# The activation of the second MoE: its series kept in the PSUM bank of h, with one SBUF input per VectorE operation

## The chip, the cores and the metric

The kernel runs on one core of a Trainium2 chip. The metric is the device time of one execution in microseconds (us), taken as the median of several runs. One execution was also recorded by the hardware profiler; all rows below come from that one. A core has TensorE (PE, matmuls; PEld is its weight loads), VectorE (DVE), ScalarE (ACT), GpSimd (POOL) and SyncE (SP, which issues DMAs). TensorE writes its results to PSUM, which has eight banks of 512 fp32 columns. In this kernel VectorE and ScalarE read and write PSUM, and GpSimd works on SBUF alone.

## The reference

An RWKV-like attention over 4 x 768 tokens feeds a first MoE with eight experts (top one of eight, ReLU), and its output x of 3072 tokens x 384 goes through a second dense block, which the change concerns:

```
def _moe2_ref(x, w_in, w_out):          # x 3072x384, w_in 384x2048, w_out 2048x384
    h = x @ w_in
    g = h - np.tanh(h)
    return (g @ w_out).astype(np.float32)
```

## The kernel before, in words

The program runs its stages one after the other: attention, routing, first MoE, second MoE. Within a stage each engine has its own queue of instructions, in the order in which the code writes them, and semaphores hold an instruction until what it needs is there.

The second MoE treats the tokens in NBK = 6 blocks (j) of BK = 512 and the 2048 hidden columns in CH2 = 16 chunks (f) of 128. So there are 96 chunks, i = 16 j + f. Matrices are held as a rounded part and a remainder ("hi" and "lo"), and a product takes three passes: hi with hi, and the two mixed ones. For chunk i:

- nm1(i), L1229: nine matmuls of 512 columns into h, one whole PSUM bank (pool psh, three banks).
- in the same function ScalarE computes z = h squared (L1233), tanh(h) into t (L1235), s (L1237) and mk (L1239), which is the ReLU of z - 0.16 and serves as a mask.
- gfun(i), five VectorE operations. For small h, tanh cancels, so a series in z is used there: L1245 w = h z; L1246 t = tanh(h) - h; L1247 and L1248 multiply w by two factors, from s and from z; L1249 puts t over w where the mask is set. All values are negative g; the sign is turned at the output.
- gsplit(i): ScalarE casts w to the hi part of g (L1264), GpSimd subtracts for the lo part (L1265).
- nm2(i, q, pass), L1276: for four token tiles q, three passes, twelve matmuls of 384 columns into the accumulators o (pool pso, five banks).

Step i of the loop writes, in this order: in three steps of a block (f = 10, 11, 12) xsplit, which prepares the next block's tokens (a ScalarE cast L904, a subtraction L905); gsplit(i + 1); nm1(i + 3); in the first eight steps w_split, which prepares the last weights (L84 on ScalarE, L85 on GpSimd); nm2; at a block's end o_copy (L1282 on VectorE for the first tile, L1284 on ScalarE for the others); gfun(i + 3); in four steps of a block a scatter of the block before (L1289, an indirect DMA that GpSimd issues). In the last block four nm2 are held back (HELD), to be done after the loop. After the loop the remaining nm2 run in two parts, tile by tile, and behind each tile of the second part stand its o_copy and scatter.

Three banks of h mean that nm1(i + 3) writes the bank of chunk i and waits until its last reader has ended. That is L1246 here, the second operation of gfun. The tiles z, t, s, mk and w have two buffers each.

Before the second MoE, the first one has a "decode" (L936 to L943), which unpacks the second MoE's weights on VectorE, partly in a PSUM tile of 384 columns named dec: L938 reads and writes dec in place, L940 reads it and writes SBUF.

Of the kernel before, what the change touches and what calls it, by code (L numbers as in the profile page):

```python
# [8 lines left out]
F32 = mybir.dt.float32  # L9
# [3 lines left out]
U32 = mybir.dt.uint32  # L13
U64 = mybir.dt.uint64
ACTF = mybir.ActivationFunctionType
ALU = mybir.AluOpType
# [6 lines left out]
G_T = 0.4  # L23
G_A = 2.6447346478370597
G_B = -0.0715155286080183
G_D = 6.5360647804198555
G_K = 0.01926817304071779
# [3 lines left out]
def rwkv_moe_moe_kernel(ctx: ExitStack, tc: tile.TileContext, rk_t, rkv, pk, u, wp1, wp2, out):  # L31


    nc = tc.nc
    B, C, P, _, H, D = rkv.shape
# [43 lines left out]
    def w_split(p, part, eng=nc.vector):  # L79
        half, n = part // 2, 384  # L80
        sl = slice(part * n, (part + 1) * n)
        of = stg[p, half][:, part % 2 * n:(part % 2 + 1) * n]
        dst = ring[p % RING]
        nc.scalar.copy(out=dst[:, 0, sl], in_=of)  # L84
        eng.tensor_tensor(out=dst[:, 1, sl], in0=of, in1=dst[:, 0, sl].bitcast(F32), op=ALU.subtract)  # L85
        if part % 2:
            stg.pop((p, half))

    def w1_of(i):
        p, c = divmod(i, 2)  # L90
        W = ring[p % RING]
        return lambda s, kk: W[:, s, kk * 256 + c * P:kk * 256 + (c + 1) * P]
# [39 lines left out]
    gt2 = const.tile([P, 1], F32, name="gt2")  # L132
# [11 lines left out]
    def consts():  # L144
        nc.gpsimd.memset(ones16, 1.0)
        nc.gpsimd.memset(gb, G_K ** 0.5 * G_B)
        nc.gpsimd.memset(gt2, -G_T * G_T)
        nc.gpsimd.tensor_copy(out=ltri, in_=mlt)
        nc.gpsimd.iota(out=iotaf, pattern=[[1, P]], base=-P, channel_multiplier=0,
                       allow_small_or_imprecise_dtypes=True)  # L150
        nc.gpsimd.iota(out=pid, pattern=[[1, 1]], base=0, channel_multiplier=1,
                       allow_small_or_imprecise_dtypes=True)
        nc.gpsimd.iota(out=e8, pattern=[[-1, E]], base=E, channel_multiplier=0,
                       allow_small_or_imprecise_dtypes=True)
        nc.gpsimd.iota(out=thr, pattern=[[P, 4]], base=0, channel_multiplier=0,
                       allow_small_or_imprecise_dtypes=True)
        nc.gpsimd.iota(out=q1, pattern=[[1, 4]], base=1, channel_multiplier=0,
                       allow_small_or_imprecise_dtypes=True)
        nc.gpsimd.iota(out=ide, pattern=[[1, E]], base=0, channel_multiplier=0,
                       allow_small_or_imprecise_dtypes=True)  # L160
        nc.gpsimd.iota(out=iov, pattern=[[P, QOV]], base=0, channel_multiplier=0,
                       allow_small_or_imprecise_dtypes=True)
        for e in range(E):
            nc.gpsimd.memset(capv[:, e:e + 1], float(CAPS[e]))

        nc.gpsimd.iota(out=tie, pattern=[[-1, E]], base=0, channel_multiplier=0,
                       allow_small_or_imprecise_dtypes=True)
        nc.gpsimd.memset(tie[:, 0:1], float(2 * N * E))

        nc.gpsimd.iota(out=tileid, pattern=[[P, NT]], base=0, channel_multiplier=0,  # L170
                       allow_small_or_imprecise_dtypes=True)
# [489 lines left out]
    with tc.manual_schedule():  # L661
# [101 lines left out]
        for q in range(2):  # L763
            t = ps1.tile([P, HP, P], F32, tag=f"A{q}", name=f"hp{q}").rearrange("p j t -> p (j t)")
# [129 lines left out]
    BK = 512  # L894
# [3 lines left out]
    def x_tile(name):  # L898
        return xbp.tile([P, 2, KD, BK], F32R, tag="xb", name=name)

    def xsplit(j, d, eng=nc.vector):
        if d == 0:
            xb[j] = x_tile("xb")
        nc.scalar.copy(out=xb[j][:, 0, d, :], in_=Y[d][:, j * BK:(j + 1) * BK])  # L904
        eng.tensor_tensor(out=xb[j][:, 1, d, :], in0=Y[d][:, j * BK:(j + 1) * BK],  # L905
                          in1=xb[j][:, 0, d, :].bitcast(F32), op=ALU.subtract)
# [234 lines left out]
    with tc.manual_schedule():  # L1141
# [7 lines left out]
        for i in range(NC1):  # L1149
# [9 lines left out]
            e, f = divmod(i, CH1)  # L1159
# [8 lines left out]
            for t in range(*((max(k, 0) * NT // S0) for k in (i - CH1, i - CH1 + 1))):  # L1168
                if t < NT:
                    nc.gpsimd.indirect_dma_start(  # L1170
                        out=permd, out_offset=bass.IndirectOffsetOnAxis(ap=pos[:, t:t + 1], axis=0),
                        in_=tok[:, t:t + 1], in_offset=None)
            if i == CH1 + S0 + 2:
                nc.gpsimd.dma_start(out=perm, in_=permd.rearrange("(i p) o -> p (i o)", p=P))
            if i == CH1 + S0 + 4:
# [3 lines left out]
                                        op0=ALU.logical_shift_right, op1=ALU.bitwise_and)  # L1179
                nc.vector.tensor_scalar(out=pc, in0=perm, scalar1=9, scalar2=7,  # L1180
                                        op0=ALU.logical_shift_right, op1=ALU.logical_shift_left)
# [23 lines left out]
    hz, gg, ops, osb = {}, {}, {}, {}  # L1205
    m2 = ctx.enter_context(ExitStack())
    with tc.manual_schedule():

        wl = x_tile("wl").rearrange("p s k t -> p (s k t)").bitcast(F32)
        for k in range(LATE):  # L1210
            w = wl[:, k * 1536:(k + 1) * 1536]
# [4 lines left out]
    gsp = m2.enter_context(tc.tile_pool(name="gsp", bufs=2))  # L1216
# [5 lines left out]
    def nm1(i):  # L1222
        j, f = divmod(i, CH2)
        wf = w1_of(NC1 + f)
        ps = psh.tile([P, BK], F32, tag="h", name="h")
        n = 0
        for kk in range(KD):
            for a, b in PASS:
                nc.tensor.matmul(ps, lhsT=wf(a, kk), rhs=xb[j][:, b, kk, :], start=(n == 0), stop=(n == 8))  # L1229
                n += 1  # L1230

        z = gsp.tile([P, BK], F32, tag="z", name="z")
        nc.scalar.activation(out=z, in_=ps, func=ACTF.Square)  # L1233
        t = gsp.tile([P, BK], F32, tag="t", name="t")
        nc.scalar.activation(out=t, in_=ps, func=ACTF.Tanh)  # L1235
        s = gsp.tile([P, BK], F32, tag="s", name="s")
        nc.scalar.activation(out=s, in_=z, func=ACTF.Square, scale=G_K ** 0.5, bias=gb)  # L1237
        mk = gsp.tile([P, BK], F32, tag="mk", name="mk")
        nc.scalar.activation(out=mk, in_=z, func=ACTF.Relu, bias=gt2)  # L1239
        hz[i] = ps, z, s, t, mk  # L1240

    def gfun(i):
        ps, z, s, t, mk = hz.pop(i)
        ww = gsp.tile([P, BK], F32, tag="w", name="w")
        nc.vector.tensor_tensor(out=ww, in0=ps, in1=z, op=ALU.mult)  # L1245
        nc.vector.tensor_tensor(out=t, in0=t, in1=ps, op=ALU.subtract)  # L1246
        nc.vector.scalar_tensor_tensor(out=ww, in0=s, scalar=G_K * G_D, in1=ww, op0=ALU.add, op1=ALU.mult)  # L1247
        nc.vector.scalar_tensor_tensor(out=ww, in0=z, scalar=G_A, in1=ww, op0=ALU.subtract, op1=ALU.mult)  # L1248
        nc.vector.copy_predicated(out=ww, mask=mk.bitcast(U32), data=t)  # L1249
        gg[i] = ww  # L1250

    def g_buf(i):

# [7 lines left out]
    def gsplit(i):  # L1261
        ww = gg[i]
        g = gg[i] = g_buf(i)
        nc.scalar.copy(out=g[:, 0, :], in_=ww)  # L1264
        nc.gpsimd.tensor_tensor(out=g[:, 1, :], in0=ww, in1=g[:, 0, :].bitcast(F32), op=ALU.subtract)  # L1265
# [27 lines left out]
    with tc.manual_schedule():  # L1293
        NC2 = NBK * CH2
        done = 0
        for i in range(LEAD):
            if i == LEAD - 1:
                gsplit(0)
            nm1(i)
            gfun(i)  # L1300
        for i in range(NC2):
            j, f = divmod(i, CH2)
            if f in (10, 11, 12) and j + 1 < NBK:
                xsplit(j + 1, f - 10, nc.gpsimd if j == 0 else nc.vector)
            if i + 1 < NC2:
                gsplit(i + 1)
            if i + LEAD < NC2:
                nm1(i + LEAD)
            if i < 4 * LATE:
                w_split(NP1 + NP2 - LATE + i // 4, i % 4, eng=nc.gpsimd)  # L1310
            if j < NBK - 1 or (f not in HELD and i + LEAD < NC2):

                if f == 0:
                    for q in range(NQ2):
                        nm2(done, q, (0, 1))
                    for q in range(NQ2):
                        nm2(done, q, (2,))
                elif f == CH2 - 1:
                    for q in range(NQ2):
                        nm2(done, q, (0, 1, 2))  # L1320
                    o_copy(j, 0, True)
                else:
                    for n in range(3):
                        for q in range(NQ2):
                            nm2(done, q, (n,))
                done += 1
            if i + LEAD < NC2:
                gfun(i + LEAD)
            if f == CH2 - 1 and j < NBK - 1:
                for q in range(1, NQ2):  # L1330
                    o_copy(j, q, False)
            if j > 0 and f in (1, 2, 3, 4):
                scatter(j - 1, f - 1)

        for part in (range(done, NC2 - 2), range(NC2 - 2, NC2)):
            for q in range(NQ2):
                for i in part:
                    nm2(i, q, (0, 1, 2))
                if part[-1] == NC2 - 1:
                    o_copy(NBK - 1, q, q % 2 == 0)  # L1340
                    scatter(NBK - 1, q)
# [50 lines left out]
```

## Time and profile before

| | us |
|---|---|
| median of 3 runs | 853.72 (852.47 to 856.5) |
| profiled execution | 846.33 |
| its span, first to last instruction | 844.6 |
| PE busy / PEld busy | 793.5 (94%) / 702.8 (83%) |
| DVE busy | 716.6 (85%) |
| ACT busy / POOL busy | 529.5 (63%) / 442.9 (52%) |

The span is what lies between the first and the last instruction of the profiled execution. PE's busy time is modelled from matmuls that overlap each other; the starts of its weight loads, one for each matmul, show its pace better. Shares are means over stages which have different limits, so what counts is read stage by stage. The second MoE's first matmul is at 410.40 us.

### The profile page before, as it was taken

To read this page: it belongs to the slowest core of one execution; us is meant where nothing else is said; L and a number is where in the kernel's file an instruction comes from. 1 tells how busy PE (TensorE), PEld (TensorE's weight loads), DVE (VectorE), ACT (ScalarE), POOL (GpSimd) and SP (SyncE) were. 2 spreads that over 40 slices of the span, in tenths; PEclk is the share of its full clock that TensorE was granted. 3 is DMA by queue.
4 is the path that set the end of the run, shared out by engine and by line. 5 is a ranking of instruction groups with operands and counts; after the bars stand their busy time and mean duration, and the time that the engine had idled before them with its cause. 6 is when DMAs were issued, how large, how long until landed. Compare 5 with 4: busy or idle time off the path is not lost.

```text
span 844.6 us, 14609 instructions
## 1 busy us (share of the span) xinstructions
PE 793.5 (94%) x5052; PEld 702.8 (83%) x5052; DVE 716.6 (85%) x1139; ACT 529.5 (63%) x1135; POOL 442.9 (52%) x426
## 2 busy tenths in 40 slices
PE   8799999899999899998998989999999999999985
PEld 7567777798899899998977779989989989988875
DVE  7798887459867869896499999999999999999992
ACT  7778786336444435544566676777777677677660
POOL 6997785237577677666344534325325334334433
PEclk8999999999999999999999999999999999999998
DMA  8978863246688799885200000000000000000000
GB/s 220 272 213 222 255 183 105 84 129 197 184 268 238 207 250 285 241 238 136 88 1 1 1 10 29 1 0 38 1 1 38 1 0 29 10 1 19 20 1 37
DMA packets 34982, 89.91 MB, mean 106 GB/s; under 512 B 5690, under 2 KB 13022, under 8 KB 34896
## 3 DMA queue, kind: packets, MB, share of 16 engines
q1 hardware_dynamic: 30704, 78.87, 32.6%
q0 software_dynamic: 4192, 9.99, 3.7%
q8 instruction: 42, 0.69, 0.3%
q14 instruction: 44, 0.36, 0.1%
HBM read 73.10 MB, written 15.74 MB: 105 GB/s over the span
## 4 chain that ended last, share of the span: by engine, by line
DVE 27%; issue 11%; ACT 7%; PE 7%; POOL 1%; DVEq 0%; POOLq 0%; ACTq 0%
DVE w L1247 12%; DVE w L1248 6%; DVE w L1245 5%; PE h L1229 3%; DVE w L1249 2%; PE o L1276 2%; ACT mk L1239 2%; PE y L1004 1%; ACT z L1233 1%; ACT g L1264 1%; ACT s L1237 1%; PE hps L979 1%; ACT t L1235 1%; ACT xb L904 1%; DVE xb L905 1%
## 5 line engine op out<-in xcount | busy, mean ns | idle before, releaser
L1265 POOL TENSOR_TENSOR g<-w,g 128x512 fp32r<-128x512 f32 x93 | 121.7, 1308 | 232.5 <-ACT g L1264 220.4
L1229 PE MATMUL h<-xb,ring 128*128 128x512 f32 x864 | 217.6, 396 | 6.6 <-DVE xb L905 3.5
L1276 PE MATMUL o<-ring,g 128*128 128x384 f32 x1116 | 211.6, 338 | 6.9 <-ACT g L1264 3.9
L1276 PEld LDWEIGHTS o<-ring,g 128*128 128x128 f32 x1116 | 195.8, 188 | 19.4 <-ACT g L1264 8.0
L1229 PEld LDWEIGHTS h<-xb,ring 128*128 128x128 f32 x864 | 160.7, 188 | 40.1 <-DVE xb L905 5.2
L1247 DVE SCALAR_TENSOR_TENSOR w<-s,w 128x512 f32<-128x512 f32 x96 | 138.4, 1441 | 0.0
L85 POOL TENSOR_TENSOR ring<-stg,ring 128x384 fp32r<-128x384 f32 x102 | 105.3, 1057 | 47.8 <-ACT ring L84 38.6
L1264 ACT CAST g<-w 128x512 fp32r<-128x512 f32 x93 | 57.9, 622 | 110.4 <-DVE w L1249 110.4
L1004 PE MATMUL y<-h,ring 128*128 128x256 f32 (+7 forms) x576 | 115.5, 345 | 1.3 <-DVE h L983 1.1
L979 PE MATMUL hps<-xt,ring 128*128 128x472 f32 (+6 forms) x504 | 107.1, 355 | 5.8 <-DVE xt L968 3.1
L1004 PEld LDWEIGHTS y<-h,ring 128*128 128x128 f32 x576 | 102.2, 190 | 5.2 <-DVE h L983 1.4
L84 ACT CAST ring<-stg 128x384 fp32r<-128x384 f32 x152 | 71.8, 511 | 55.3 <-DMA stg<-in_wp_dram 40.4
L979 PEld LDWEIGHTS hps<-xt,ring 128*128 128x128 f32 x504 | 90.8, 189 | 10.9 <-DVE xt L968 3.7
L1249 DVE COPY_PREDICATED w<-mk,t 128x512 f32<-128x512 uint32 x96 | 80.1, 835 | 9.9
L1248 DVE SCALAR_TENSOR_TENSOR w<-z,w 128x512 f32<-128x512 f32 x96 | 68.4, 713 | 3.3
L1245 DVE TENSOR_TENSOR w<-h,z 128x512 f32<-128x512 f32 x96 | 65.3, 680 | 6.8 <-ACT t L1235 6.8
L1237 ACT ACTIVATE s<-z,gb 128x512 f32<-128x512 f32 x96 | 69.5, 724 | 0.0
L1239 ACT ACTIVATE mk<-z,gt 128x512 f32<-128x512 f32 x96 | 69.2, 721 | 0.0
L1246 DVE TENSOR_TENSOR t<-t,h 128x512 f32<-128x512 f32 x96 | 65.2, 679 | 0.0
L1233 ACT ACTIVATE z<-h 128x512 f32<-128x512 f32 x96 | 57.2, 595 | 11.1 <-PE h L1229 10.1
L344 ACT ACTIVATE am<-ident,dt 128x128 f32<-128x128 f32 x192 | 58.6, 390 | 4.9 <-DVE dt L337 4.5
L983 DVE SCALAR_TENSOR_TENSOR h<-hps,h 128x256 fp32r<-128x256 f32 (+7 forms) x64 | 35.9, 563 | 25.9 <-ACT h L982 25.2
(233 smaller groups left out, 1111.3 us busy)
## 6 DMA issues: line engine op xcount, KB each, us to landing
stg<-in_wp_dram SPq DMA_DIRECT2D x64, 384.0 KB
n<-in_rkv_dram SPq DMA_DIRECT2D x24, 576.0 KB
d<-in_wp_dram SPq DMA_DIRECT2D x32, 384.0 KB
t<-in_rk_t_dram SPq DMA_DIRECT2D x48, 192.0 KB
wdec<-dcf SPq DMA_DIRECT2D x32, 192.0 KB
xd<-xs SPq DMA_DIRECT2D x24, 192.0 KB
stg<-wdec SPq DMA_DIRECT2D x12, 384.0 KB
wl<-wdec SPq DMA_DIRECT2D x2, 768.0 KB
```

The lines of the kernel that those rows point to most:

```text
L85: eng.tensor_tensor(out=dst[:, 1, sl], in0=of, in1=dst[:, 0, sl].bitcast(F32), op=ALU.subtract)
L979: nc.tensor.matmul(ps, lhsT=wf(a, kk), rhs=xt[e][b][:, kk, :], start=(n == 0), stop=(n == 8))
L1004: nc.tensor.matmul(yps[d], lhsT=wf(a)[:, d * P:(d + 1) * P], rhs=h2[:, b, :], start=(f == 0 and n == 0), stop=(f == CH1 - 1 and n == 2))
L1229: nc.tensor.matmul(ps, lhsT=wf(a, kk), rhs=xb[j][:, b, kk, :], start=(n == 0), stop=(n == 8))
L1237: nc.scalar.activation(out=s, in_=z, func=ACTF.Square, scale=G_K ** 0.5, bias=gb)
L1239: nc.scalar.activation(out=mk, in_=z, func=ACTF.Relu, bias=gt2)
L1245: nc.vector.tensor_tensor(out=ww, in0=ps, in1=z, op=ALU.mult)
L1247: nc.vector.scalar_tensor_tensor(out=ww, in0=s, scalar=G_K * G_D, in1=ww, op0=ALU.add, op1=ALU.mult)
L1248: nc.vector.scalar_tensor_tensor(out=ww, in0=z, scalar=G_A, in1=ww, op0=ALU.subtract, op1=ALU.mult)
L1249: nc.vector.copy_predicated(out=ww, mask=mk.bitcast(U32), data=t)
L1265: nc.gpsimd.tensor_tensor(out=g[:, 1, :], in0=ww, in1=g[:, 0, :].bitcast(F32), op=ALU.subtract)
L1276: nc.tensor.matmul(ops[q], lhsT=gg[i][:, b, q * P:(q + 1) * P], rhs=wf(a), start=(f == 0 and n == 0), stop=(f == CH2 - 1 and n == 2))
```

## The change

The two SBUF inputs of the last three operations of gfun become one. The series is formed in the bank of h itself: L1245 now subtracts (t and h), L1246 multiplies h by z in place, L1247 and L1248 go on in place, and the predicated copy (now L1250) puts the series over t where the mask is set. For that the mask is turned round (0.16 - z), t takes the place of w and gets three buffers, and w is gone. The tile h is then read up to the last operation. The subtraction of xsplit runs on GpSimd for all blocks and not for the first alone. The second of the two last parts of nm2 takes three chunks and not two.

```
-        nc.gpsimd.memset(gt2, -G_T * G_T)
+        nc.gpsimd.memset(gt2, G_T * G_T)
...
-        t = gsp.tile([P, BK], F32, tag="t", name="t")
+        t = gsp.tile([P, BK], F32, tag="t", name="t", bufs=3)
         nc.scalar.activation(out=t, in_=ps, func=ACTF.Tanh)
...
-        nc.scalar.activation(out=mk, in_=z, func=ACTF.Relu, bias=gt2)
+        nc.scalar.activation(out=mk, in_=z, func=ACTF.Relu, scale=-1.0, bias=gt2)
...
     def gfun(i):
         ps, z, s, t, mk = hz.pop(i)
-        ww = gsp.tile([P, BK], F32, tag="w", name="w")
-        nc.vector.tensor_tensor(out=ww, in0=ps, in1=z, op=ALU.mult)
         nc.vector.tensor_tensor(out=t, in0=t, in1=ps, op=ALU.subtract)
-        nc.vector.scalar_tensor_tensor(out=ww, in0=s, scalar=G_K * G_D, in1=ww, op0=ALU.add, op1=ALU.mult)
-        nc.vector.scalar_tensor_tensor(out=ww, in0=z, scalar=G_A, in1=ww, op0=ALU.subtract, op1=ALU.mult)
-        nc.vector.copy_predicated(out=ww, mask=mk.bitcast(U32), data=t)
-        gg[i] = ww
+        nc.vector.tensor_tensor(out=ps, in0=ps, in1=z, op=ALU.mult)
+        nc.vector.scalar_tensor_tensor(out=ps, in0=s, scalar=G_K * G_D, in1=ps, op0=ALU.add, op1=ALU.mult)
+        nc.vector.scalar_tensor_tensor(out=ps, in0=z, scalar=G_A, in1=ps, op0=ALU.subtract, op1=ALU.mult)
+
+        nc.vector.copy_predicated(out=t, mask=mk.bitcast(U32), data=ps)
+        gg[i] = t
...
-                xsplit(j + 1, f - 10, nc.gpsimd if j == 0 else nc.vector)
+                xsplit(j + 1, f - 10, nc.gpsimd)
...
-        for part in (range(done, NC2 - 2), range(NC2 - 2, NC2)):
+        for part in (range(done, NC2 - 3), range(NC2 - 3, NC2)):
```

On VectorE, one chunk of gfun stands like this in the kernel before (h is the PSUM bank; the other names are tiles in SBUF; what an instruction waits for is in brackets):

```order
L1245 TENSOR_TENSOR w<-h,z 128x512 [waits Activation_49,Pool_49]
L1246 TENSOR_TENSOR t<-t,h 128x512
L1247 SCALAR_TENSOR_TENSOR w<-s,w 128x512 [waits DVE_49,Activation_49]
L1248 SCALAR_TENSOR_TENSOR w<-z,w 128x512 [waits DVE_49]
L1249 COPY_PREDICATED w<-mk,t 128x512 [waits DVE_49,Activation_49]
```

And like this in the changed kernel:

```order
L1245 TENSOR_TENSOR t<-t,h 128x512 [waits Activation_49]
L1246 TENSOR_TENSOR h<-h,z 128x512
L1247 SCALAR_TENSOR_TENSOR h<-s,h 128x512 [waits DVE_49,Activation_49]
L1248 SCALAR_TENSOR_TENSOR h<-z,h 128x512 [waits DVE_49]
L1250 COPY_PREDICATED t<-mk,h 128x512 [waits DVE_49,Activation_49]
```

The number of operations is the same. L1247 now waits for the operation right before it, where it waited for the one before that; the wait for GpSimd has moved from VectorE to ScalarE's tanh, which writes t.

On GpSimd, from the last scatter of block 0 to the first of block 1 (g is the split activation, xb the split tokens, Y the first MoE's output, osb the output tile), the kernel before has:

```order
L1289 DMA out_dram<-osb,perm 3072x384
L1265 TENSOR_TENSOR g<-w,g 128x512 [waits PE_49,Activation_49] x13
L1289 DMA out_dram<-osb,perm 3072x384 [waits DMASW3_49]
```

The changed kernel has there:

```order
L1290 DMA out_dram<-osb,perm 3072x384
L1266 TENSOR_TENSOR g<-t,g 128x512 [waits PE_49,Activation_49,Pool_49] x5
L905 TENSOR_TENSOR xb<-Y_4170,xb 128x512 [waits Activation_49]
L1266 TENSOR_TENSOR g<-t,g 128x512 [waits PE_49,Activation_49,Pool_49]
L905 TENSOR_TENSOR xb<-Y_4171,xb 128x512 [waits Activation_49]
L1266 TENSOR_TENSOR g<-t,g 128x512 [waits PE_49,Activation_49,Pool_49]
L905 TENSOR_TENSOR xb<-Y_4172,xb 128x512 [waits Activation_49]
L1266 TENSOR_TENSOR g<-t,g 128x512 [waits PE_49,Activation_49,Pool_49] x6
L1290 DMA out_dram<-osb,perm 3072x384 [waits DMASW3_49]
```

Three subtractions have come between those of g, and the same in each of the blocks 1 to 4; they have left VectorE's queue.

## Rows read from the trace of the kernel before

**Rows 1.** Single lines: count, duration in ns (min/median/max), first and last start, form.

```profile
L1246 DVE TENSOR_TENSOR t<-t,h x96: 665/678/708, 414.6 to 823.4; 128x512 f32<-128x512 f32 x96
...
L1247 DVE SCALAR_TENSOR_TENSOR w<-s,w x96: 682/1554/1584, 415.2 to 824.0; 128x512 f32<-128x512 f32 x96
...
L1249 DVE COPY_PREDICATED w<-mk,t x96: 727/758/1795, 416.7 to 826.3; 128x512 f32<-128x512 uint32 x96
...
L359 DVE COPY_PREDICATED am<-mlt,A x48: 705/721/743, 16.2 to 147.6; 128x512 f32<-128x512 uint32 x48
...
L938 DVE SCALAR_TENSOR_TENSOR dec<-d,dec x32: 561/562/564, 220.4 to 377.9; 128x384 int32<-128x384 int32 x32
...
L940 DVE SCALAR_TENSOR_TENSOR dca<-d,dec x32: 553/553/555, 220.9 to 378.5; 128x384 int32<-128x384 int32 x32
...
L905 DVE TENSOR_TENSOR xb<-Y,xb x15: 669/678/1332, 395.5 to 755.1; 128x512 fp32r<-128x512 f32 x15
L905 POOL TENSOR_TENSOR xb<-Y,xb x3: 1288/1830/1871, 469.4 to 478.9; 128x512 fp32r<-128x512 f32 x3
```

**Rows 2.** Timeline of VectorE, first chunk: start, duration, instruction, [idle before, releaser].

```profile
414.00 0.69 DVE L1245 TENSOR_TENSOR w<-h,z 128x512 f32<-128x512 f32 x1 [6.82 <-ACT t L1235]
...
415.20 0.68 DVE L1247 SCALAR_TENSOR_TENSOR w<-s,w 128x512 f32<-128x512 f32 x1
415.92 0.69 DVE L1248 SCALAR_TENSOR_TENSOR w<-z,w 128x512 f32<-128x512 f32 x1
...
417.35 0.69 DVE L1245 TENSOR_TENSOR w<-h,z 128x512 f32<-128x512 f32 x1
```

**Rows 3.** Timeline, GpSimd and VectorE in a later chunk.

```profile
488.97 1.30 POOL L1265 TENSOR_TENSOR g<-w,g 128x512 fp32r<-128x512 f32 x1 [2.92 <-ACT g L1264]
489.27 1.54 DVE L1247 SCALAR_TENSOR_TENSOR w<-s,w 128x512 f32<-128x512 f32 x1
...
490.85 0.69 DVE L1248 SCALAR_TENSOR_TENSOR w<-z,w 128x512 f32<-128x512 f32 x1
```

**Rows 4.** Timeline of TensorE's weight loads in the second MoE.

```profile
410.40 8.30 PEld L1229 LDWEIGHTS h<-xb,ring 128*128 128x128 f32 x36
...
432.33 2.05 PEld L1276 LDWEIGHTS o<-ring,g 128*128 128x128 f32 x12 [0.94 <-ACT g L1264]
...
480.81 0.30 PEld L1229 LDWEIGHTS h<-xb,ring 128*128 128x128 f32 x2 [1.08 <-POOL xb L905]
...
483.29 2.00 PEld L1229 LDWEIGHTS h<-xb,ring 128*128 128x128 f32 x9
...
497.10 1.68 PEld L1276 LDWEIGHTS o<-ring,g 128*128 128x128 f32 x10 [2.62 <-DVE osb L1282]
...
502.94 2.00 PEld L1229 LDWEIGHTS h<-xb,ring 128*128 128x128 f32 x9
504.98 2.16 PEld L1276 LDWEIGHTS o<-ring,g 128*128 128x128 f32 x12
507.12 2.00 PEld L1229 LDWEIGHTS h<-xb,ring 128*128 128x128 f32 x9
...
552.11 0.30 PEld L1229 LDWEIGHTS h<-xb,ring 128*128 128x128 f32 x2 [1.66 <-DVE xb L905]
...
795.94 2.00 PEld L1229 LDWEIGHTS h<-xb,ring 128*128 128x128 f32 x9
...
830.14 4.17 PEld L1276 LDWEIGHTS o<-ring,g 128*128 128x128 f32 x24
```

**Rows 5.** The page's list of lines: busy us, mean ns of one, idle before.

```profile
L1237 ACT ACTIVATE s<-z,gb 128x512 f32<-128x512 f32 x96 | 69.5, 724 | 0.0
```

**Rows 6.** Timeline of the end, GpSimd and ScalarE.

```profile
832.39 0.99 POOL L1289 DMA_INDIRECT out_dram<-osb,perm  x1 [3.21 <-DVE osb L1282]
...
834.67 0.49 ACT L1284 ACTIVATE osb<-o 128x384 f32<-128x384 f32 x1 [1.59 <-PE o L1276]
...
836.24 0.97 POOL L1289 DMA_INDIRECT out_dram<-osb,perm  x1 [0.30 <-issue]
```

## The prediction

> **What bounds the kernel now.** I read three views of the second MoE, the only stage that the change touches: single lines of VectorE over all chunks, the timeline of VectorE beside GpSimd, and TensorE's weight loads.
>
> The first chunk shows VectorE alone, since GpSimd has nothing yet: gfun begins at 414.00 and the next chunk's at 417.35, so five operations take 3.35 us [rows 2]. Later, L1247 begins 0.30 us after GpSimd's subtraction and ends at 490.81, 0.54 us after that one's end at 490.27 [rows 3]: it stands still until GpSimd is done, and then takes its usual time. Its median over 96 chunks is 1.554 us, against 0.682 at best [rows 1], so the stall is 0.87 and a chunk costs VectorE 3.35 + 0.87 = 4.22. L1249 shows the same in the steps where GpSimd also splits weights (up to 1.795). L1246, with one input in PSUM and one in SBUF, never passes 0.708 [rows 1]. The reader is to see that the stall goes with two SBUF inputs.
>
> TensorE in its steady stretch needs 2.04 us for a chunk's first product (502.94 to 504.98) and 2.14 for the second (504.98 to 507.12): 4.18 a chunk, with no gap [rows 4]. So two engines stand level, 4.22 and 4.18, and a faster VectorE can only win what TensorE waits. For 96 chunks TensorE needs 401.3. It takes from 410.40 to 834.31 (830.14 + 4.17), which is 423.9 [rows 4]. The waits are 22.6 us in all:
> - from 410.40 to 483.29, 17 first and 14 second products need 64.6 of 72.9: 8.3 waited, nearly 1 us in each of the weight-splitting steps (0.94 at 432.33) and some at block 0's end (1.08 at 480.81).
> - from 483.29 to 502.94, four of each need 16.7 of 19.6: 2.9, mostly the one wait of 2.62 for VectorE's o_copy.
> - four later block ends, where TensorE waits for VectorE's L905 (1.66 at 552.11, and three of about 1.2 that look like it): net of what the loads catch up, 4.5.
> - the rest, 6.9, lies after 795.94, where the last block's held products are missing between the first ones and VectorE can't follow.
>
> **The change part by part.**
>
> The new gfun: five operations of the same length, each with one SBUF input. I take 0.87 off. L1247 now follows the operation that it waits for; the pair L1247, L1248 in that position is 0.72 apart (415.20 to 415.92), where operations without such a wait follow in 0.60 (two steps from 414.00 to 415.20) [rows 2], so I add 0.12. In-place work in PSUM: the decode's L938, in place, takes 562 ns against 553 for L940, which writes SBUF, so 0.01 for each of three operations. The predicated copy from PSUM has a twin in attention, L359: 0.721 against L1249's 0.758 [rows 1], so nothing. Sum 3.35 + 0.12 + 0.03 = 3.50 us a chunk. Bounds: 3.3 (the old chunk without stall, the copy a little shorter) and 4.37 (3.50 and one stall of 0.87 left in the copy, whose mask and destination are both in SBUF).
>
> [...]
>
> So VectorE drops to 84% of TensorE's 4.18, and TensorE sets the pace. ScalarE and GpSimd have less to do in a chunk than either: GpSimd 1.30 [rows 3].
>
> xsplit on GpSimd: 12 subtractions leave VectorE (0.678 each) and come to GpSimd at 1.288 when not disturbed [rows 1]. [...] In the loop's order the third subtraction stands one step before the product that needs it, and that product needs it only for its eighth matmul. Counted from the start of step 11's first product, that matmul is due 2 x 4.18 + 1.6 = 9.9 later. The subtraction is done 2.1 (product) + 4 x 0.72 (ScalarE's four, none longer than L1237 [rows 5]) + 0.6 (cast) + 1.3 = 6.9 later, once ScalarE no longer waits for a late VectorE. That leaves 3 us, so the 4.5 at block ends go. Bounds: all 4.5 stay, or all go; I take all gone.
>
> The start: 8.3 waited become 1.0. The bank of h is now held to the end of gfun. The fourth first product wants bank 0 at 410.40 + 3/4 x 8.30 = 416.6 [rows 4]; the changed gfun of chunk 0 runs from 414.00 to about 417.6 (3.50, and 0.1 until the copy's end). So TensorE waits 1.0 there, once: from then on three chunks of TensorE are 12.5 us, and a bank is held some 7 (the product 2.1, then 1.5 until gfun begins, as from 412.5 to 414.00 in chunk 0, gfun 3.5). Behind the waiting matmul stands nm2(0), which nothing but TensorE's own queue delays. The rest of the 8.3 goes, since 3.50 leaves VectorE faster than TensorE even in the weight-splitting steps, when GpSimd can't hold it up any more. Bounds: 0 to 1.5 for the wait.
>
> [...] By the rows the longer hold costs the 1.0 above, and more only where VectorE falls behind, which is the second rival.
>
> o_copy (2.9) goes: it waited in a VectorE queue that lagged. The tanh's new wait on GpSimd, three chunks back, ends a step before tanh is due; behind it stand only that chunk's s and mask. The turned mask is the same ScalarE operation.
>
> The tail: with held products left out, TensorE's mean step is (4.18 + 4.18 + 2.04) / 3 = 3.47, and VectorE's 3.50 falls only 0.03 a chunk behind, within some 3 us of slack. The last gfun ends some 8.5 us after the last first product begins, its lo part 2 us later; the 48 matmuls of the first part cover 4.2 + 8.5 us by then. So the 6.9 go. With nine matmuls to a tile in the second part (24 loads in 4.17, so 1.56 a tile) the four scatters no longer queue at 1.28 apart (832.39 to 836.24 in three intervals): the last began 1.08 after its copy's end (834.67 + 0.49), and would begin 0.3 after it: 0.8 won [rows 4, 6].
>
> Sum: 22.6 - 1.0 - 0.2 (the first 0.2 us of the stretch, which nothing touches) + 0.8 = 22.2 us. The span of 844.6 becomes 822.4, the profiled execution's 846.3 becomes 824.1. The shown runs have a median of 853.7, 7.4 above the profiled one; taking the saving off it gives 831.5.
>
> **The rivals.**
>
> Waits of latency stay. If TensorE's waits at block ends (4.5) and in the tail (6.9) come from the path through ScalarE and GpSimd rather than from a late VectorE, they remain, and the held bank adds to them. For it: block 0, where GpSimd already did xsplit, waited as well (1.08 at 480.81). Against it: there GpSimd's 1.83 was VectorE's doing. Time: 831.5 + 4.5 + 6.9 = 843.
>
> Slower: the stall moves to another operation. If the predicated copy, which writes t in SBUF and reads the mask there, is still held by GpSimd, VectorE needs 3.50 + 0.87 = 4.37 for each of 96 chunks. Before, its gfuns ran from 414.00 to 827.1 (826.3 and the copy's length [rows 1, 2]), 413.1 us, o_copies and xsplits among them; with 3.3 for the o_copies, which remain, it breaks even at (413.1 - 3.3) / 96 = 4.27 a chunk. At 4.37 the end comes 9.6 later, less 0.8 at the tail: 862.5. Against it: L359, of this very form, never passes 0.743 in 48 calls [rows 1].
>
> The change doesn't do what it says: if the stall has nothing to do with the count of SBUF inputs, L1247 keeps 1.55, TensorE's waits stay, and the time is 853.7 + 1.0 - 0.8 = 854. Against it: L1246 under the same GpSimd work.
>
> **How the numbers follow.** Forecast 0.80 (831.5, own range 827 to 836); waits stay 0.12 (843); no effect 0.04 (854); slower 0.04 (862.5). The range 827 to 842 takes in the bounds of the start and of the block ends and half of the second case. A measurement of this kernel can tell about 0.5%, 4.3 us, from no change. Faster by more than that: the first two, 0.92; within: 0.04; slower: 0.04.
>
> **What would show it.** Right: L1247 near 0.69 in all chunks; gfun 3.5 us long; weight loads at 4.18 a chunk from about 420 to the end, with gaps of under 0.2 at block ends; one wait of about 1 us near 416.6 for the copy L1250; GpSimd's subtractions all at 1.3; the last scatter 0.3 after its copy. Wrong: any gfun operation with a median over 0.9, a wait of TensorE for h (L1250) or xb (L905) that recurs, or loads that need more than 4.18 without a wait.

## The result and the profile after

The changed kernel takes 830.21 us (median of 4 runs, 827.69 to 831.18) against 853.1 (4 runs, 850.82 to 856.5) for the kernel before, timed beside it: a ratio of 0.972, 95% interval 0.968 to 0.976. The forecast was 831.5, with a chance of 0.92 for faster.

The second MoE is the stage that was changed. From TensorE's first weight load to the end of its last it took 423.91 us before [rows 4]; now:

```profile
416.65 6.20 PEld L1229 LDWEIGHTS h<-xb,ring 128*128 128x128 f32 x27
423.95 1.93 PEld L1229 LDWEIGHTS h<-xb,ring 128*128 128x128 f32 x9 [1.10 <-DVE t L1250]
425.93 2.16 PEld L1277 LDWEIGHTS o<-ring,g 128*128 128x128 f32 x12
...
545.11 2.00 PEld L1229 LDWEIGHTS h<-xb,ring 128*128 128x128 f32 x9
547.15 2.16 PEld L1277 LDWEIGHTS o<-ring,g 128*128 128x128 f32 x12
549.29 2.00 PEld L1229 LDWEIGHTS h<-xb,ring 128*128 128x128 f32 x9
...
817.83 1.05 PEld L1277 LDWEIGHTS o<-ring,g 128*128 128x128 f32 x6
```

That is the timeline of the weight loads (start, duration, instruction, count, [idle before, releaser]). From 416.65 to 818.88 it takes 402.23, 21.7 less. The one wait left in the whole stage is 1.10 at 423.95, for the copy that gives back the first bank of h. The product at 545.11 is the one (chunk 32's) that waited 1.66 at a block's end before, for its last two loads [rows 4]; now its nine loads run on, and the next first product begins 4.18 later.

The profiled execution has a span of 828.4, only 16.2 less, because its first stages, which the change doesn't touch, ended 6.25 later than in the profile of before (416.65 against 410.40). That is scatter: over all profiles here, the second MoE began between 408.8 and 416.65, whatever the kernel, while its length came out the same within 0.3 for the same kernel. So small differences between kernels are read here from the length of the stage, and the timed ratios decide on the whole.

VectorE in the first chunk, answering to [rows 2]:

```profile
420.24 0.69 DVE L1245 TENSOR_TENSOR t<-t,h 128x512 f32<-128x512 f32 x1 [6.82 <-ACT t L1235]
420.85 0.69 DVE L1246 TENSOR_TENSOR h<-h,z 128x512 f32<-128x512 f32 x1
421.64 0.70 DVE L1247 SCALAR_TENSOR_TENSOR h<-s,h 128x512 f32<-128x512 f32 x1
422.37 0.69 DVE L1248 SCALAR_TENSOR_TENSOR h<-z,h 128x512 f32<-128x512 f32 x1
423.17 0.73 DVE L1250 COPY_PREDICATED t<-mk,h 128x512 f32<-128x512 uint32 x1
423.79 0.67 DVE L1245 TENSOR_TENSOR t<-t,h 128x512 f32<-128x512 f32 x1
```

From 420.24 to 423.79 a chunk is 3.55. And the single lines over all chunks (ns min/median/max, first and last start), answering to [rows 1]:

```profile
L1247 DVE SCALAR_TENSOR_TENSOR h<-s,h x96: 696/696/697, 421.6 to 807.9; 128x512 f32<-128x512 f32 x96
L1248 DVE SCALAR_TENSOR_TENSOR h<-z,h x96: 695/695/696, 422.4 to 808.7; 128x512 f32<-128x512 f32 x96
L1250 DVE COPY_PREDICATED t<-mk,h x96: 726/750/768, 423.2 to 809.5; 128x512 f32<-128x512 uint32 x96
...
L905 POOL TENSOR_TENSOR xb<-Y,xb x15: 1293/1305/1308, 466.9 to 742.8; 128x512 fp32r<-128x512 f32 x15
```

L1247 had 1.554 in the middle and 1.584 at most; now its 96 durations lie within 1 ns. GpSimd's share of xsplit is at its undisturbed 1.3. The copy, whose mask and destination are in SBUF, isn't held even where it runs beside GpSimd's subtraction (timelines of GpSimd and of VectorE):

```profile
451.02 1.31 POOL L1266 TENSOR_TENSOR g<-t,g 128x512 fp32r<-128x512 f32 x1
```

```profile
451.64 0.77 DVE L1250 COPY_PREDICATED t<-mk,h 128x512 f32<-128x512 uint32 x1
```

The two overlap from 451.64 to 452.33, and the copy takes its 0.77. Most copies begin only just before GpSimd ends; of the 96, five begin 0.2 us or more before that end, and none of the five takes longer than 0.77.

The chain that ended last, shares of the span by engine, then by line:

```profile
PE 48%; DVE 2%; issue 1%; POOL 1%; ACT 0%; POOLq 0%; DVEq 0%; ACTq 0%
PE h L1229 23%; PE o L1277 22%; PE y L1004 2%; PE hps L979 1%; DVE t L1250 0%; DVE h L1247 0%; DVE h L1248 0%; DVE h L1246 0%; DVE t L1245 0%; POOL out_dram L1290 0%; POOL g L1266 0%; ACT g L1265 0%; POOLq L1388 0%; ACT z L1233 0%; ACT t L1235 0%
```

The two products of the second MoE now are 45% of the span, and gfun's lines have fallen to 0% of the chain. VectorE waits instead, 0.5 us a chunk for the tanh, which costs nothing. The end, answering to [rows 6] (timeline of ScalarE and GpSimd):

```profile
819.25 0.49 ACT L1285 ACTIVATE osb<-o 128x384 f32<-128x384 f32 x1 [2.63 <-PE o L1277]
820.01 0.97 POOL L1290 DMA_INDIRECT out_dram<-osb,perm  x1 [0.52 <-issue]
```

The last scatter begins 0.27 after its copy ends (819.74), where it began 1.08 after it; from the last load to the span's end it is 9.5 against 10.3.

### The profile page after: what moved, and what is told of

It is laid out like the page before. It is cut to its first block, busy times and chain, and to the rows that moved or that the text cites. A ratio compares the mean times of both kernels' runs of the same rounds, so it can differ in the third digit from the quotient of the medians.

```text
span 828.4 us, 14436 instructions
## 1 busy us (share of the span) xinstructions
PE 788.7 (95%) x5052; PEld 704.7 (85%) x5052; DVE 649.7 (78%) x1127; ACT 525.5 (63%) x1135; POOL 449.3 (54%) x438
## 4 chain that ended last, share of the span: by engine, by line
PE 48%; DVE 2%; issue 1%; POOL 1%; ACT 0%; POOLq 0%; DVEq 0%; ACTq 0%
PE h L1229 23%; PE o L1277 22%; PE y L1004 2%; PE hps L979 1%; DVE t L1250 0%; DVE h L1247 0%; DVE h L1248 0%; DVE h L1246 0%; DVE t L1245 0%; POOL out_dram L1290 0%; POOL g L1266 0%; ACT g L1265 0%; POOLq L1388 0%; ACT z L1233 0%; ACT t L1235 0%
## 5 line engine op out<-in xcount | busy, mean ns | idle before, releaser
L1266 POOL TENSOR_TENSOR g<-t,g 128x512 fp32r<-128x512 f32 x93 | 120.4, 1295 | 176.3 <-ACT g L1265 121.3
L1277 PE MATMUL o<-ring,g 128*128 128x384 f32 x1116 | 209.3, 336 | 0.0
L85 POOL TENSOR_TENSOR ring<-stg,ring 128x384 fp32r<-128x384 f32 x102 | 105.8, 1060 | 50.9 <-ACT ring L84 41.1
L979 PEld LDWEIGHTS hps<-xt,ring 128*128 128x128 f32 x504 | 92.3, 191 | 10.3 <-DVE xt L968 3.4
L1245 DVE TENSOR_TENSOR t<-t,h 128x512 f32<-128x512 f32 x96 | 65.8, 685 | 43.0 <-ACT t L1235 42.8
L1250 DVE COPY_PREDICATED t<-mk,h 128x512 f32<-128x512 uint32 x96 | 72.2, 753 | 9.9
L1247 DVE SCALAR_TENSOR_TENSOR h<-s,h 128x512 f32<-128x512 f32 x96 | 66.9, 696 | 10.0
L1248 DVE SCALAR_TENSOR_TENSOR h<-z,h 128x512 f32<-128x512 f32 x96 | 66.8, 695 | 3.3
L1246 DVE TENSOR_TENSOR h<-h,z 128x512 f32<-128x512 f32 x96 | 66.5, 693 | 0.0
L1265 ACT CAST g<-t 128x512 fp32r<-128x512 f32 x93 | 57.6, 619 | 8.0 <-DVE t L1250 5.8
L85 DVE TENSOR_TENSOR ring<-stg,ring 128x384 fp32r<-128x384 f32 x50 | 40.1, 803 | 23.8 <-ACT ring L84 23.4
```

What stands on the lines that cost most here:

```text
L979: nc.tensor.matmul(ps, lhsT=wf(a, kk), rhs=xt[e][b][:, kk, :], start=(n == 0), stop=(n == 8))
L1247: nc.vector.scalar_tensor_tensor(out=ps, in0=s, scalar=G_K * G_D, in1=ps, op0=ALU.add, op1=ALU.mult)
L1248: nc.vector.scalar_tensor_tensor(out=ps, in0=z, scalar=G_A, in1=ps, op0=ALU.subtract, op1=ALU.mult)
L1250: nc.vector.copy_predicated(out=t, mask=mk.bitcast(U32), data=ps)
L1277: nc.tensor.matmul(ops[q], lhsT=gg[i][:, b, q * P:(q + 1) * P], rhs=wf(a), start=(f == 0 and n == 0), stop=(f == CH2 - 1 and n == 2))
```

## The experiments

The theory: VectorE was late because an operation with two SBUF inputs stands still while GpSimd subtracts; gfun's new operands end that, TensorE's waits go with it, and the other two edits matter little. The rivals: the waits at block ends and in the tail come from the path through ScalarE and GpSimd, so that moving xsplit and cutting the tail carry part of the gain; or it is in-place work, the destination in PSUM, that frees VectorE. Times are medians; "stage" is the second MoE from first to last load, as above. The kernel before was timed beside them three times, with medians of 847.5 (for e1 to e4), 850.27 (e5 to e8) and 850.51 us (e9 to e12); each ratio is against its own. Stages of 423.91 and 402.23 are the marks.

**e1, the new gfun alone.** The changed kernel with xsplit and the tail as before:

```diff
-                xsplit(j + 1, f - 10, nc.gpsimd)
+                xsplit(j + 1, f - 10, nc.gpsimd if j == 0 else nc.vector)
-        for part in (range(done, NC2 - 3), range(NC2 - 3, NC2)):
+        for part in (range(done, NC2 - 2), range(NC2 - 2, NC2)):
```

> The new gfun alone; xsplit's subtraction is back on VectorE for blocks 1 to 4 and the last part of nm2 is back at two chunks. Theory (a VectorE operation with two SBUF inputs stands still while GpSimd's subtraction runs, and the gain is what TensorE waited for the slow VectorE): VectorE needs 3.5 x 16 + 3 x 0.6 + 0.5 = 58 us of a block's 67, so L1247 stays at 0.70, TensorE's waits at the block ends (1.66 and three of 1.2 before) are gone though VectorE still does L905, and only the tail's 0.8 us is given back: second MoE from first to last weight load 402.2 (after: 402.2), time about 831. Rival (the block ends were won by moving xsplit to GpSimd): the four waits of 1.1 to 1.7 come back, about 4.5 us, time about 835.

Measured: 827.69 us, ratio 0.979 [0.974, 0.983]; the stage 402.24. Of VectorE's xsplit and of TensorE's waits (total, times, longest) the trace says:

```profile
L905 DVE TENSOR_TENSOR xb<-Y,xb x15: 669/674/1270, 394.4 to 737.2; 128x512 fp32r<-128x512 f32 x15
```

```profile
PEld h L1229 <- DVE t L1250: 1.1, 1, 1.1
```

So gfun carries all of the 21.7 in the stage. The 12 subtractions cost VectorE nothing where it has time to spare. From the last load to the end it is again 10.3: that part belongs to the split of the tail. (The ratio, 0.979, is against a kernel before that was timed at 847.5 here; the stage, not the ratio, tells e1 from the changed kernel.)

**e2, the rest alone.** The kernel before with the other two edits:

```diff
-                xsplit(j + 1, f - 10, nc.gpsimd if j == 0 else nc.vector)
+                xsplit(j + 1, f - 10, nc.gpsimd)
-        for part in (range(done, NC2 - 2), range(NC2 - 2, NC2)):
+        for part in (range(done, NC2 - 3), range(NC2 - 3, NC2)):
```

> The kernel before with xsplit's subtraction on GpSimd in all blocks and the last part of nm2 at three chunks; the old gfun. Theory: GpSimd's added subtractions meet the two-SBUF-input operations, so each costs VectorE about what it saves; block ends look like block 0's (waits of 0.9, 0.5 and 1.1), L1247 stays at 1.55, the tail's queue is 0.8 us shorter. Time 852 to 857, second MoE 422 to 428. Rival (xsplit's move and the tail carry a large part): time 845 or less, second MoE under 417.

Measured: 853.99 us, ratio 1.007 [1.004, 1.009]; the stage 427.13, 3.2 longer. TensorE's waits:

```profile
PEld o L1276 <- ACT g L1264: 10.7, 12, 2.6
PEld o L1276 <- DVE osb L1282: 8.8, 4, 2.6
PEld h L1229 <- DVE t L1246: 3.8, 2, 2.3
```

Before, the block ends waited for xsplit on VectorE:

```profile
PEld h L1229 <- DVE xb L905: 5.2, 4, 1.7
```

and once, for 2.6, for o_copy. Now they wait for o_copy (8.8), the next thing in the same late queue. Behind one of these waits (2.19, until 633.31) the nine loads of a first product took 3.29 instead of 2.00, which is part of the 3.2:

```profile
635.23 3.29 PEld L1229 LDWEIGHTS h<-xb,ring 128*128 128x128 f32 x9
```

In the tail the last chunk's g comes late, in e2 (first two lines: the last first product, the longest wait) as in the kernel before (last two):

```profile
813.50 1.93 PEld L1229 LDWEIGHTS h<-xb,ring 128*128 128x128 f32 x9 [2.29 <-DVE t L1246]
829.75 0.30 PEld L1276 LDWEIGHTS o<-ring,g 128*128 128x128 f32 x2 [2.64 <-ACT g L1264]
```

```profile
811.67 1.93 PEld L1229 LDWEIGHTS h<-xb,ring 128*128 128x128 f32 x9 [2.28 <-DVE t L1246]
819.46 0.30 PEld L1276 LDWEIGHTS o<-ring,xb 128*128 128x128 f32 x2 [1.57 <-ACT xb L1264]
```

The wait is 1.1 longer with three chunks in the second part, but from the last first product to the end of the loads e2 takes 22.4 (813.50 to 835.91) and the kernel before 22.6 (811.67 to 834.31, the stretch from 821 to 823 at a granted clock of 0.50, see the last section). From the last load to the span's end e2 takes 9.5 against 10.3. So the new tail wins its 0.8 beside the slow gfun too, and the stage's 3.2 are lost ahead of it, mostly at the block ends: moving xsplit is harmless only beside the fast gfun. The two edits were not run apart from each other.

**e3, one input of one operation.** The kernel before, but the product goes to the bank, so that L1247 reads it there; it still writes SBUF, and the copy is the old one:

```diff
-        nc.vector.tensor_tensor(out=ww, in0=ps, in1=z, op=ALU.mult)
         nc.vector.tensor_tensor(out=t, in0=t, in1=ps, op=ALU.subtract)
-        nc.vector.scalar_tensor_tensor(out=ww, in0=s, ..., in1=ww, ...)
+        nc.vector.tensor_tensor(out=ps, in0=ps, in1=z, op=ALU.mult)
+        nc.vector.scalar_tensor_tensor(out=ww, in0=s, ..., in1=ps, ...)
```

> The kernel before with a gfun in which only L1247's inputs change: t - h first, h z in place in PSUM, then L1247 reads s (SBUF) and h (PSUM) and writes w in SBUF; L1248 (z, w) and the copy (mk, t) still have two SBUF inputs; xsplit and the tail as before. Theory (inputs): L1247 goes to 0.70 although it writes SBUF as before; the stall moves to whichever of L1248 and the copy then meets GpSimd's 1.30 us, for a part of it: VectorE 3.6 to 4.2 a chunk, median of L1248 or of the copy up to 1.3; most of the gain remains, time 831 to 842. Rival (it is the writes to SBUF that meet GpSimd's writes, and PSUM outputs freed them): L1247 stays near 1.55, time 850 to 855.

Measured: 825.92 us, ratio 0.974 [0.971, 0.978]; the stage 401.31, with no wait at all. The single lines:

```profile
L1247 DVE SCALAR_TENSOR_TENSOR w<-s,h x96: 686/687/692, 418.9 to 805.5; 128x512 f32<-128x512 f32 x96
L1248 DVE SCALAR_TENSOR_TENSOR w<-z,w x96: 691/950/1808, 419.6 to 806.2; 128x512 f32<-128x512 f32 x96
```

L1247, with one SBUF input and an SBUF destination, isn't held any more: it is the inputs, not where the result goes. Nor has it slipped away from GpSimd: 51 of the 96 instances begin while a subtraction runs, and none takes over 0.692. L1248, untouched and with two SBUF inputs, has moved into GpSimd's subtraction and is held in its turn, as in a steady chunk (timelines of GpSimd and of VectorE):

```profile
563.50 1.29 POOL L1265 TENSOR_TENSOR g<-w,g 128x512 fp32r<-128x512 f32 x1 [1.27 <-ACT g L1264]
```

```profile
564.26 1.08 DVE L1248 SCALAR_TENSOR_TENSOR w<-z,w 128x512 f32<-128x512 f32 x1
```

It ends at 565.34, 0.55 after GpSimd's end at 564.79; in [rows 3] that was 0.54. It is held for less, since it begins later in the subtraction (0.76 after its start, not 0.30), and that is enough.

**e4, only the copy with two SBUF inputs.** As e3, but L1247 writes the bank and L1248 reads it there and writes ww:

```diff
-        nc.vector.scalar_tensor_tensor(out=ww, in0=s, ..., in1=ps, ...)
-        nc.vector.scalar_tensor_tensor(out=ww, in0=z, ..., in1=ww, ...)
+        nc.vector.scalar_tensor_tensor(out=ps, in0=s, ..., in1=ps, ...)
+        nc.vector.scalar_tensor_tensor(out=ww, in0=z, ..., in1=ps, ...)
```

> As the one before, but L1248 too reads h in PSUM (writing w in SBUF), so that the predicated copy alone has two SBUF inputs (mask mk and data t) and an SBUF destination; xsplit and the tail as before. Theory (inputs): the first four operations stay at 0.70, the copy stands still in a part of the chunks, as far as GpSimd's subtraction reaches it: up to 0.9 more where it starts with GpSimd's, nothing where it starts later; time 830 to 845. My slower rival of the forecast, one stall moved to the copy in every chunk (VectorE 4.37 a chunk), would give a median of the copy of 1.6 and a time of 855 to 863.

Measured: 825.36 us, ratio 0.973 [0.969, 0.977]; the stage 401.39, one wait of 0.3 for the bank.

```profile
L1249 DVE COPY_PREDICATED w<-mk,t x96: 748/763/1840, 420.2 to 806.8; 128x512 f32<-128x512 uint32 x96
```

With mask and data both in SBUF the copy can be held (1.840), but at its place in the chunk it seldom is: 11 of the 96 take over 1.0, and 51 others begin in the last 0.1 us of a subtraction, where nothing holds them (at most 0.786).

**e5 and e10, the bank given back sooner at the start.** The changed kernel with the series of chunk 0 (e5), then of chunks 0 and 1 (e10, `i < 2`) in an SBUF tile:

```diff
+        ww = gsp.tile([P, BK], F32, tag="w", name="w", bufs=1) if i == 0 else ps
-        nc.vector.tensor_tensor(out=ps, in0=ps, in1=z, op=ALU.mult)
+        nc.vector.tensor_tensor(out=ww, in0=ps, in1=z, op=ALU.mult)
... (the two operations and the copy after it likewise)
```

> The changed kernel, but chunk 0 alone forms its series in an SBUF tile, so that the bank of h is free after its second operation. Theory: the one wait that the longer hold costs (1.10 us of TensorE for L1250, before the fourth first product) is gone and nothing comes in its place: second MoE from first to last weight load 401.2 instead of 402.2, time 1 us under the changed kernel's, about 829. Rival (a wait elsewhere takes its place, since nm2(0) needs chunk 0's g, which comes no earlier): second MoE 402.2, same time.

> The changed kernel with chunks 0 and 1 in SBUF; chunk 0 alone left a wait of 0.36 for chunk 1's copy. Theory (the wait goes on to the next chunk's bank until VectorE has caught up): second MoE 401.3, no wait left. Chunk 1's operations with two SBUF inputs meet GpSimd's first subtraction and one of them stands still for up to 0.9, which TensorE doesn't see. Rival (that stall makes chunk 2 late, whose bank TensorE wants next): a wait of 0.3 to 0.9 stays, second MoE 401.6 to 402.2.

Measured: e5 825.3 us, ratio 0.971 [0.968, 0.974], the stage 401.61; e10 825.95 us, 0.973 [0.969, 0.977], the stage 401.69. In e5 the wait of 1.10 is gone, and one of 0.36 stands a chunk later:

```profile
420.60 1.93 PEld L1229 LDWEIGHTS h<-xb,ring 128*128 128x128 f32 x9 [0.36 <-DVE t L1251]
```

In e10 that one is gone too, but one of 0.43 stands another chunk later (at 424.28, for chunk 2's copy): chunk 1 now has two SBUF inputs while GpSimd subtracts for chunk 0, from 417.23 to 418.54, and VectorE's L1248, which begins at 417.71, takes 1.37:

```profile
417.71 1.37 DVE L1248 SCALAR_TENSOR_TENSOR w<-s,w 128x512 f32<-128x512 f32 x1
```

That is e10's rival. Of the 0.9 that the longer hold of the bank costs, e5 wins back 0.6, and e10 no more, because the old stall returns with the two SBUF inputs.

**e6, GpSimd only writes.** The kernel before; the second half of g is filled with zeros instead of the remainder of the split, so that the third pass of the second product adds nothing:

```diff
-        nc.gpsimd.tensor_tensor(out=g[:, 1, :], in0=ww, in1=g[:, 0, :].bitcast(F32), op=ALU.subtract)
+        nc.gpsimd.memset(g[:, 1, :].bitcast(F32), 0.0)
```

> The kernel before, in which GpSimd writes zeros to the lo part of g instead of the subtraction (so the third pass of nm2 adds nothing): it writes SBUF and reads nothing. Theory (VectorE's second SBUF input and GpSimd's reads share a way into SBUF): L1247 goes to 0.69 median with its two SBUF inputs kept, VectorE needs about 3.4 a chunk, the second MoE falls to 402 to 408. Rival (any work of GpSimd in SBUF holds such an operation): L1247 stands still for as long as the memset runs, a median over 0.9.

Measured, one execution: 824.9 us; the stage 401.30, no wait.

```profile
L1247 DVE SCALAR_TENSOR_TENSOR w<-s,w x96: 674/684/1503, 416.3 to 801.1; 128x512 f32<-128x512 f32 x96
...
L1265 POOL MEMSET g<- x93: 520/527/548, 409.2 to 798.7; 128x512 f32 x93
```

The old L1247, with both inputs in SBUF, has a median of 0.684. The four instances of about 1.50 begin beside GpSimd's weight split, L85, which still subtracts (one at 439.88, while L85 runs from 439.81 to 440.83). The timelines of GpSimd and VectorE show that L1247 does overlap with the memset:

```profile
602.24 0.53 POOL L1265 MEMSET g<- 128x512 f32 x1 [3.65 <-PE o L1276]
```

```profile
602.37 0.68 DVE L1247 SCALAR_TENSOR_TENSOR w<-s,w 128x512 f32<-128x512 f32 x1
```

Held until 602.77 and 0.54 beyond, it would end at 603.31; it ends at 603.05. So GpSimd's memset, which only writes, doesn't hold VectorE (L1247's median is 0.684 here); its subtraction, which also reads SBUF, does (1.554 before). The theory's shared way into SBUF was the author's guess: the runs show these times, not what the two engines share. The memset is also shorter (0.527 against 1.308 for the subtraction before, a mean) and waits for another engine, so the 401.30 isn't the stall's price alone.

**e11 and e12, how much slower VectorE may be.** The changed kernel with one more operation a chunk (e11), then two (e12), whose result nothing reads:

```diff
+        scr0 = gsp.tile([P, BK], F32, tag="scr0", name="scr0", bufs=1)
+        nc.vector.tensor_tensor(out=scr0, in0=z, in1=ps, op=ALU.mult)
```

> The changed kernel with one more VectorE operation in each chunk (z times h into a scratch tile that nobody reads), which takes VectorE from 3.55 to 4.15 us a chunk, just under TensorE's 4.18. Theory (TensorE sets the pace, and a VectorE faster than 4.18 is worth nothing): second MoE 402 to 406, time within 4 us of the changed kernel's although VectorE works 58 us more. Rival (the gain came from VectorE's time itself, in proportion: 16 us of it saved per 5 us gained or the like): time up by 15 us or more.

> The same with two such operations, the second behind the first on the same scratch tile: VectorE 4.85 to 4.95 a chunk, above TensorE's 4.18 and above the 4.27 at which the forecast put the break-even with the kernel before. Theory: VectorE now sets the pace, second MoE 96 x 4.9 + 8 = 475 to 485 us, time 900 to 912, slower than the kernel before (424 us) by about what 4.9 is above its 4.30. Rival (the three banks and the order of the queues hide part of it): second MoE under 460.

Measured: e11 835.79 us, ratio 0.983 [0.979, 0.988], the stage 412.33; e12 906.72 us, 1.068 [1.062, 1.073], the stage 479.94. In e11 a chunk is 4.15 on VectorE (599.84 to 603.99), still under TensorE's 4.18, and in the middle there is next to no wait. But the stage is 10 us longer than the changed kernel's, and the waits tell where most of it is:

```profile
PEld h L1229 <- DVE t L1252: 9.1, 6, 2.1
```

```profile
779.90 1.93 PEld L1229 LDWEIGHTS h<-xb,ring 128*128 128x128 f32 x9 [2.12 <-DVE t L1252]
...
792.33 1.93 PEld L1229 LDWEIGHTS h<-xb,ring 128*128 128x128 f32 x9 [2.13 <-DVE t L1252]
...
804.78 1.93 PEld L1229 LDWEIGHTS h<-xb,ring 128*128 128x128 f32 x9 [2.15 <-DVE t L1252]
```

7.2 of the 9.1 lie in the last block, where held products are left out and TensorE's mean step is 3.47: one wait of 2.1 in every three chunks, near the 2.0 that VectorE lacks there (3 x 4.15 less 3 x 3.47). My expectation, a stage of 402 to 406, forgot this; the rival, 15 us or more, was not met either. In e12 VectorE needs 4.85 and the time follows it; 71 of the first products wait for it, most of them like these:

```profile
603.93 1.93 PEld L1229 LDWEIGHTS h<-xb,ring 128*128 128x128 f32 x9 [0.72 <-DVE t L1254]
605.91 2.16 PEld L1281 LDWEIGHTS o<-ring,g 128*128 128x128 f32 x12
608.78 1.93 PEld L1229 LDWEIGHTS h<-xb,ring 128*128 128x128 f32 x9 [0.72 <-DVE t L1254]
```

**e7 and e8, both kernels again.** No edit.

> The kernel before, profiled once more. The forecast took the saving off the median of the runs, since the profiled execution was 7.4 us below it. If that was luck of the first 410 us (attention and first MoE, which wait for DMAs), this profile's second MoE begins about 417 and lasts 424 again from first to last weight load, with a time near 853. Rival: the second MoE itself varies by several us from run to run, and its length here differs from 423.9 by over 2.

> The changed kernel once more, beside the one with chunk 0 in SBUF. Second MoE 402.2 from first to last weight load as in its first profile; its start, which the change doesn't touch, anywhere from 410 to 418 us (410.40 in the profile of before, 416.65 in that of the changed kernel). Time 828 to 832.

Measured: e7, one execution, 849.9 us, the stage 424.2, begun at 413.70 and not at 417; e8 828.61 us, ratio 0.975 [0.973, 0.978], the stage 402.23. The stages repeat within 0.3 us; what varies is when they begin.

**e9, the smallest edit with the new tail.** e3 and three chunks in the tail's second part:

```diff
-        for part in (range(done, NC2 - 2), range(NC2 - 2, NC2)):
+        for part in (range(done, NC2 - 3), range(NC2 - 3, NC2)):
```

> The gfun in which only L1247's inputs change (its run had 401.31 us of second MoE and no wait of TensorE), with the last part of nm2 at three chunks. The bank of h is free after L1247 and not after the copy. Theory: second MoE 401.3 from first to last weight load, 0.9 less than the changed kernel, and the same 9.5 us from there to the end: 0.9 us under the changed kernel. Rival (VectorE, at 93% in the middle of the stage against the changed kernel's 83%, falls behind in the last block, and the earlier second part then waits for the last chunk's g): a wait of 0.5 us or more behind 800, second MoE 402 or more.

Measured: 825.2 us, ratio 0.972 [0.968, 0.976]; the stage 401.30, 9.5 from the last load to the end. The first four products run through with no wait for the bank:

```profile
413.98 8.30 PEld L1229 LDWEIGHTS h<-xb,ring 128*128 128x128 f32 x36
422.32 2.16 PEld L1276 LDWEIGHTS o<-ring,g 128*128 128x128 f32 x12
```

401.3 is 96 times 4.18: this stage is TensorE's own time. By the profiles e9 is 0.9 better than the changed kernel; the timed ratios, 0.972 and 0.975, have intervals that overlap and don't tell them apart.

## Why the prediction was right

- **What bounds it.** Right. The two engines stood level, and only TensorE's waits could be won. 22.6 of them were counted and 1.10 is left; the stage lost 21.7, and 21.4 were forecast (22.6 less 1.0 and 0.2).
- **The cause of the stall.** Right, and shown rather than inferred: one input of one operation ends it (e3), an untouched operation takes it over when it slides under GpSimd's subtraction (e3, e10), and it is gone when GpSimd doesn't read (e6). L1246 was thinner evidence than it looked: only 16 of its 96 instances begin while GpSimd subtracts, where 95 of L1247's do; those 16 take at most 0.701. The 1.795 of L1249 was put down to weight splitting, but that instance began at 473.69, beside GpSimd's xsplit (473.58 to 474.86); the eight beside weight splits took 1.55 to 1.57.
- **3.50 for the new gfun.** It is 3.55. The step that was mis-sized is the one for L1247, which I took to follow 0.72 after the operation that it waits for; it follows 0.79 later (420.85 to 421.64). Worth nothing, since TensorE needs 4.18. By the rows, L1247 and L1248 in PSUM take 0.696 and 0.695, against 0.684 and 0.692 in SBUF and not held (e6), so in-place work in PSUM costs about a hundredth at most, as forecast.
- **The bank held longer.** Forecast 1.0 once, measured 1.10 once, at the fourth product.
- **xsplit on GpSimd and the 4.5 at block ends.** The sum was right, but I listed the 4.5 under this edit; e1 shows that gfun wins them by itself. e2 shows what the edit does beside the old gfun: the wait goes over to o_copy. GpSimd's subtraction for xsplit had a median of 1.831 beside the old gfun (e2) and has 1.305 beside the new one.
- **The tail.** The 6.9 and the 0.8 came as forecast: the 6.9 by gfun alone (e1), the 0.8 by the split (10.3 in e1, 9.5 with it). One term was mis-sized: the last gfun ended 10.2 us after the last first product began (800.07 to 810.22), where 8.5 was forecast, and its lo part 12.3 after it, just inside the 12.7 that the first part was to cover. It cost nothing.
- **The time.** 831.5 forecast, 830.21 measured. The profiled span was forecast at 822.4 and came out at 828.4, since the first stages ended 6.25 later, and the rest won 0.3 more than forecast. That the time agrees within 1.3 us is partly luck, since the kernel before had medians from 847.5 to 853.7 us; the ratio is the firmer number, 0.974 forecast (831.5 to 853.7), 0.972 measured, and 0.975 in e8.
- **The rivals.** Waits of latency: none stayed. No effect: no. The slower one, the copy held in every chunk: its maximum is 0.768. Its break-even, 4.27 a chunk, fits the runs all the same: between 4.15 (stage 412.3) and 4.85 (479.9) a straight line passes 424 at 4.27, an estimate. But its price, 0.87 in each chunk, would have been too high: in e4 the copy with two SBUF inputs has a median of 0.763, because when one operation is no longer held, the others move against GpSimd's subtraction, and most copies begin at its very end.

## What to carry to other kernels

Where two engines stand level, count what the one waits for the other: that is all a faster partner can win, and an operand moved to another memory may win it whole. Look at the stretch where the pace is highest, here the last block at 3.47 a chunk: it wants more slack than the steady part, and a lag of 0.7 a chunk there cost 7 us in e11. An edit that is free beside a fast engine can cost beside a slow one, as xsplit's move does in e2, so test the parts of a change apart before crediting one.

## What the runs showed of the hardware

- An operation of VectorE with two SBUF inputs that is held by GpSimd's subtraction ended, in the instances read here, about the same time after it, wherever it began: L1247 and L1248 0.54 to 0.55 (e3, e10, [rows 3]), the predicated copy 0.62 (kernel before: GpSimd's end at 474.86, the copy's at 475.48). So the price depends on when the two meet: a held operation that came 0.46 later lost that much less (1.08 in e3, 1.54 in [rows 3]), and those that began in the last 0.1 us lost nothing (L1247 at 471.18 and 480.72 in the kernel before, 0.71 each; 51 copies of e4, at most 0.786).
- TensorE's granted clock fell once in the tail of the kernel before, from 1.00 to 0.50, after TensorE had been busy 7.34 of 11 us; in the changed kernel's tail, busy throughout, it stayed at 1.00. Rows of stretches, two of before and one of after (length, busy of PE, PEld, DVE, ACT and POOL, granted clock, DMA share, GB/s):

```profile
810.00:821.00 11.00, 7.34 (x36) 6.29 (x37) 10.72 (x14) 7.87 (x15) 3.87 (x3) 0.98 0.00 0
821.00:823.00 2.00, 2.00 (x7) 2.00 (x8) 1.86 (x4) 0.64 (x2) 0.00 (x0) 0.50 0.00 0
```

```profile
800.00:818.00 18.00, 18.00 (x101) 17.50 (x101) 10.37 (x17) 7.14 (x13) 7.15 (x6) 1.00 0.03 11
```

  Six matmuls of the second product took 2.12 us there and 1.20 at a granted clock of 1.00, the first row from before, the second from after:

```profile
821.30 2.12 PE L1276 MATMUL o<-ring,g 128*128 128x384 f32 x6
```

```profile
816.44 1.20 PE L1277 MATMUL o<-ring,g 128*128 128x384 f32 x6
```

  The nine loads behind those six took 2.05, against 1.57 for the same nine a tile later (825.98). TensorE waits for nothing there, so about 1.4 of the 6.9 lost in the tail was clock, an estimate from these rows; by their order in time it followed the waits: 2.28 until 811.67 and 1.57 until 819.46, then a mean clock of 0.75 from 820 to 821.
